# One ordered block for attention and experts, weight sums on VectorE, token copies on two engines

## The chip, the cores and the metric

The kernel runs on one core of a Trainium2 chip. A core has five engines with their own instruction lists: TensorE (PE, with its weight loads PEld), VectorE (DVE), ScalarE (ACT), GpSimd (POOL) and SyncE (SP, which here issues transfers). Each engine works through its list in order and waits on semaphores for the others.

The metric is the time of one execution on the device, in microseconds (us). Before the change it is 823.42 us, the median of three runs (822.31 to 827.64).

## The reference

An attention block feeds a mixture of experts, all in float32:

```python
# attention: 8 batches x 8 heads, 576 positions, head size 64, a sliding window of 128, a bias by distance
scores = q @ k.T / sqrt(64)
attn = softmax(where(0 <= rel < 128, scores - slope_h * rel, -1e9))
x = (attn @ v)              # laid out as 4608 tokens x 512
# experts: each token goes to the one expert with the largest logit
logits = x @ w_gate         # 512 x 8
expert = argmax(logits); gate = softmax(logits)[expert]
out[token] = gate * (relu(x[token] @ w1[expert]) @ w2[expert])   # w1: 512 x 1024, w2: 1024 x 512, per expert
```

## The kernel before

**Attention.** A loop over 32 steps (batch and pair of heads) computes scores on PE, exponentials on ACT, a product with a table of factors on DVE, sums of neighbouring blocks (`mg`) on POOL, and the values on PE. Tasks for the gate run beside it: they turn the logits, choose each token's expert (`pick`), give it a row number (`place`), and `scatter` writes the token's row to a list in memory by expert. The loop stands in a block of its own, `with tc.manual_schedule()`, inside which each engine's list follows the order of the program. What stands outside such a block, or in another one, may be ordered against it by the scheduler.

**Experts.** Each of the eight experts has a big group (512 tokens) and, between two experts, a small group (128 tokens) takes tokens that did not fit: big 0, small 0, big 1, small 1, up to big 7. A big group's two matrix products use Strassen's algorithm in the form with seven products and fifteen sums: `seven1` for w1 (two halves, seven products each), `seven2` for w2. It needs sums of the blocks of the weights (`w1_sums`, `w2_sums`: four instructions of 128 x 1024 each), of the tokens (`x_sums`) and of the hidden values (`left_sums` at the end of a half). Before the change the weight sums are on GpSimd:

```python
def left_sums(eng, s, a11, a12, a21, a22):
    eng.tensor_add(s[0], a21, a22)
    eng.tensor_sub(s[1], s[0], a11)
    eng.tensor_sub(s[2], a11, a21)
    eng.tensor_sub(s[3], a12, s[1])
# right_sums: the same with four subtractions
def w1_sums(g):
    ...
    left_sums(nc.gpsimd, ...)        # w2_sums: right_sums(nc.gpsimd, ...)

def seven(order, prod, post, banks):
    where = {1: 0, 2: 0, 6: 1, 5: 1, 3: 1, 7: 2, 4: 2}   # product -> PSUM bank a, b or c
    for n in order:
        prod(n, banks[where[n]], n in (1, 6, 7))         # PE, adds to what the bank holds
        post(n, *banks)                                  # DVE or ACT reads the bank

def post(n, ba, bb, bc):             # in seven1
    if n == 1:   nc.scalar.copy(p1[:], ba[:])
    elif n == 2: nc.scalar.activation(c11, ba[:], AF.Relu)
    elif n == 6: nc.vector.tensor_add(u2[:], bb[:], p1[:])
    elif n == 5: nc.vector.tensor_add(u4[:], bb[:], p1[:]); nc.vector.tensor_add(c22, bc[:], u4[:]); ...
    elif n == 3: nc.vector.tensor_add(c12, bb[:], p1[:]); ...
    elif n == 4: nc.vector.tensor_add(c21, bc[:], u2[:]); ...; left_sums(nc.vector, hs, c11, c21, c12, c22)
```

The gathered tokens (`xg`) are turned on PE, four transposes per tile of 128 tokens, into a PSUM tile `tp` that has two buffers, and copied to `xgT` by DVE:

```python
def tokens(g):                       # where each row of the group goes in the output: two small integer operations
    nc.vector.tensor_tensor(g["si"][:, :n], bits[:, :n, Dm], g["mask"][:, 0, :], op=ALU.bitwise_and)
    nc.vector.tensor_tensor(g["si"][:, :n], g["si"][:, :n], g["mask"][:, 1, :], op=ALU.bitwise_or)

def turn(g, tiles):
    for j in tiles:
        tp = pools["ps"].tile([P, DB, P], F32, name="tp")
        for db in range(DB):
            nc.tensor.transpose(tp[:, db, :], g["xg"][:, j, db * P : (db + 1) * P], ident[:])
        nc.vector.tensor_copy(g["xT"][:, :, j * P : (j + 1) * P], tp[:])
```

The loop over the groups (cut):

```python
def experts(first):
    ...
    g = groups[0]; gather(g); ...
    w1_sums(g)
    extras()                         # counts per expert, masks, lists of the small groups: 31 short DVE instructions
    get_w1(groups[1])
    for i, g in enumerate(groups):
        after = groups[i + 1 : i + 3] + [None, None]
        if after[0] is not None:
            gather(after[0]); after[0]["w2"] = load_w2(...)
        if g["n"] == NJ:             # a big group
            ...
            if i == 0:
                turn(g, [0, 1])
                # product 1 of both halves, product 2 of both halves
                turn(g, [2, 3]); x_sums(g)
                order = (6, 7, 5, 3, 4)
            w2_sums(g)
            for half in range(2):
                seven1(g, half, order, banks[half], us[half])
            if i == 0:
                check_range(first)
        else:
            layer1(g)                # a small group: plain products
        tokens(g)
        if after[1] is not None:
            get_w1(after[1])         # load the w1 of the group after the next
        if after[0] is not None:
            turn(after[0], range(after[0]["n"]))
            if after[0]["n"] == NJ:
                x_sums(after[0])
                w1_sums(after[0])    # on GpSimd, while a small group is worked on
        if g["n"] == NJ:
            seven2(g)
        else:
            layer2(g)

with moe_pools(), tc.manual_schedule():
    experts(True)
```

Of the kernel before, what the change touches and what calls it, by code (L numbers as in the profile page):

```python
# [8 lines left out]
F32 = mybir.dt.float32  # L9
# [12 lines left out]
def kernel(  # L22
# [310 lines left out]

# [7 lines left out]
    with tc.tile_pool(name="tab", bufs=1) as tab, \  # L346
# [230 lines left out]
                ts.append(lambda i=i: (send(tiles, i - 2), row(tiles, i)))  # L577
            return ts + [lambda: [send(tiles, i) for i in (len(tiles) - 2, len(tiles) - 1)]]

        with tc.manual_schedule():  # L580
            load(0)
            load(1)
            start_routing()
            tasks = []

            def do(n):
                for task in tasks[:n]:
                    task()
                del tasks[:n]

            for u in range(NU + 1):
                b, hp = divmod(u, HP)

                slow = u < 7
                if u < NU:
                    if hp == 1 and 1 < b + 1 < NB:
                        load(b + 1)
                    if 0 < u <= E:
                        clear_rows(u - 1)
                    if u == NU // 2:  # L600
                        expert_w[0] = load_w1(moe_w1[0]), load_w2(moe_w2[0])
                    scores(u)
                    factors(u, 0)
                do(0 if slow else 1)
                if u < NU:
                    factors(u, 1)
                    merge(u)
                if u > 0:
                    values(u - 1, 0)
                    values(u - 1, 1)  # L610
                    totals(u - 1)
                    if hp == 0:
                        tasks += tasks_of(b - 1)
                do(len(tasks) if u == NU else 0 if slow else 2 if len(tasks) < 14 else 3)

# [115 lines left out]
        return st  # L733

    def bank(i):
        return pools["ps"].tile([P, 2, TH], F32, name="abc"[i % 3])

    def left_sums(eng, s, a11, a12, a21, a22):
        eng.tensor_add(s[0], a21, a22)
        eng.tensor_sub(s[1], s[0], a11)  # L740
        eng.tensor_sub(s[2], a11, a21)
        eng.tensor_sub(s[3], a12, s[1])

    def right_sums(eng, t, b11, b12, b21, b22):
        eng.tensor_sub(t[0], b12, b11)  # L745
        eng.tensor_sub(t[1], b22, t[0])  # L746
        eng.tensor_sub(t[2], b22, b12)
        eng.tensor_sub(t[3], b21, t[1])

    def w1_sums(g):  # L750
        w1 = g["w1"]
        s = g["w1s"] = pools["s"].tile([P, 4, DH, F // 2], F32, name="w1s")
        f0, f1 = slice(0, F // 2), slice(F // 2, F)
        left_sums(
            nc.gpsimd, [s[:, i] for i in range(4)],
            w1[:, :DH, f0], w1[:, DH:, f0], w1[:, :DH, f1], w1[:, DH:, f1],
        )

    def w2_sums(g):
        w2 = g["w2"]  # L760
        t = g["w2s"] = pools["s"].tile([P, 4, FH, Dm // 2], F32, name="w2s")
        right_sums(
            nc.gpsimd, [t[:, i] for i in range(4)], w2[:, :FH, lo], w2[:, :FH, hi], w2[:, FH:, lo], w2[:, FH:, hi],
        )

    def seven(order, prod, post, banks):


        where = {1: 0, 2: 0, 6: 1, 5: 1, 3: 1, 7: 2, 4: 2}
        for n in order:  # L770
            prod(n, banks[where[n]], n in (1, 6, 7))
            post(n, *banks)

    def mms(out_of, lhs, rhs, nk, first):
        for i in range(2):
# [3 lines left out]
                    stop=(k == nk - 1), skip_group_check=True,  # L779
                )  # L780

    def seven1(g, half, order, banks, us):
        w1, s, xT, t, h, hs = g["w1"], g["w1s"], g["xT"], g["xTs"], g["h"], g["hs"]
        fs = [(2 * half + i) * P for i in range(2)]
        p1, u2, u4 = us
        r0, r1 = slice(2 * half, 2 * half + 2), slice(FH + 2 * half, FH + 2 * half + 2)
        c11, c12, c21, c22 = h[:, r0, lo], h[:, r0, hi], h[:, r1, lo], h[:, r1, hi]
        sides = {
            1: (lambda i, k: w1[:, k, fs[i] : fs[i] + P], lambda k: xT[:, k, lo]),
            2: (lambda i, k: w1[:, DH + k, fs[i] : fs[i] + P], lambda k: xT[:, DH + k, lo]),  # L790
            3: (lambda i, k: s[:, 3, k, fs[i] : fs[i] + P], lambda k: xT[:, DH + k, hi]),
            4: (lambda i, k: w1[:, DH + k, F // 2 + fs[i] : F // 2 + fs[i] + P], lambda k: t[:, 3, k, :]),
            5: (lambda i, k: s[:, 0, k, fs[i] : fs[i] + P], lambda k: t[:, 0, k, :]),
            6: (lambda i, k: s[:, 1, k, fs[i] : fs[i] + P], lambda k: t[:, 1, k, :]),
            7: (lambda i, k: s[:, 2, k, fs[i] : fs[i] + P], lambda k: t[:, 2, k, :]),
        }

        def prod(n, out_of, first):
            mms(out_of, *sides[n], DH, first)

        def post(n, ba, bb, bc):
            if n == 1:
                nc.scalar.copy(p1[:], ba[:])
            elif n == 2:
                nc.scalar.activation(c11, ba[:], AF.Relu)
            elif n == 6:
                nc.vector.tensor_add(u2[:], bb[:], p1[:])
            elif n == 5:
                nc.vector.tensor_add(u4[:], bb[:], p1[:])
                nc.vector.tensor_add(c22, bc[:], u4[:])  # L810
                nc.scalar.activation(c22, c22, AF.Relu)
            elif n == 3:
                nc.vector.tensor_add(c12, bb[:], p1[:])
                nc.scalar.activation(c12, c12, AF.Relu)
            elif n == 4:
                nc.vector.tensor_add(c21, bc[:], u2[:])
                nc.scalar.activation(c21, c21, AF.Relu)

                left_sums(nc.vector, [hs[:, i, r0, :] for i in range(4)], c11, c21, c12, c22)

        seven(order, prod, post, banks)

    def temps():
        return [pools["u"].tile([P, 2, TH], F32, name=n) for n in ("p1", "u2", "u4")]

    def seven2(g):
        w2, t, h, hs = g["w2"], g["w2s"], g["h"], g["hs"]
        p1, u2, u4 = temps()
        zo = g["zo"]
# [18 lines left out]

        def post(n, ba, bb, bc):
            if n == 1:  # L850
                nc.scalar.copy(p1[:], ba[:])
            elif n == 2:
                weigh(0, 0, ba)
            elif n == 6:
                nc.vector.tensor_add(u2[:], bb[:], p1[:])
            elif n == 5:
                nc.vector.tensor_add(u4[:], bb[:], p1[:])
                nc.vector.tensor_add(o[:, 1, 1], bc[:], u4[:])  # L858
                weigh(1, 1, o[:, 1, 1])
            elif n == 3:  # L860
                nc.vector.tensor_add(o[:, 0, 1], bb[:], p1[:])
                weigh(0, 1, o[:, 0, 1])
                send_out(g, 0, zo[:, 0, :])
                send_out(g, 1, zo[:, 1, :])
            elif n == 4:
                nc.vector.tensor_add(o[:, 1, 0], bc[:], u2[:])
                weigh(1, 0, o[:, 1, 0])
                send_out(g, 2, zo[:, 2, :])
                send_out(g, 3, zo[:, 3, :])

        seven((1, 6, 7, 5, 2, 3, 4), prod, post, [bank(i) for i in range(3)])

    def send_out(g, j, row):
        ins = nc.gpsimd.indirect_dma_start(  # L874
# [19 lines left out]
        nc.vector.tensor_tensor(g["si"][:, :n], bits[:, :n, Dm], g["mask"][:, 0, :], op=ALU.bitwise_and)  # L894
        nc.vector.tensor_tensor(g["si"][:, :n], g["si"][:, :n], g["mask"][:, 1, :], op=ALU.bitwise_or)  # L895

    def turn(g, tiles):
        if tiles[0] == 0:
            g["xT"] = pools["wk"].tile([P, DB, NJ * P], F32, name="xgT")
        for j in tiles:  # L900
            tp = pools["ps"].tile([P, DB, P], F32, name="tp")
            for db in range(DB):
                nc.tensor.transpose(tp[:, db, :], g["xg"][:, j, db * P : (db + 1) * P], ident[:])  # L903
            nc.vector.tensor_copy(g["xT"][:, :, j * P : (j + 1) * P], tp[:])  # L904

    def x_sums(g):
        xT = g["xT"]
        t = g["xTs"] = pools["wk"].tile([P, 4, DH, TH], F32, name="xTs")
        right_sums(
            nc.vector, [t[:, i] for i in range(4)], xT[:, :DH, lo], xT[:, :DH, hi], xT[:, DH:, lo], xT[:, DH:, hi],  # L910
        )

    def hidden(g):
        g["h"] = pools["wk"].tile([P, FB, NJ * P], F32, name="h_sb")
# [40 lines left out]
    def experts(first):  # L955
# [12 lines left out]
        else:  # L968
            get_w1(g)
            g["w2"] = load_w2(g["src"][1])  # L970
        w1_sums(g)
        extras()
        get_w1(groups[1])
        for i, g in enumerate(groups):
            after = groups[i + 1 : i + 3] + [None, None]
# [3 lines left out]
            if g["n"] == NJ:  # L979
# [2 lines left out]
                hidden(g)  # L982
                order = (1, 6, 7, 5, 2, 3, 4)
                if i == 0:
                    turn(g, [0, 1])
                    g["xTs"] = None
                    for half in range(2):
                        seven1(g, half, (1,), banks[half], us[half])
                    for half in range(2):
                        seven1(g, half, (2,), banks[half], us[half])  # L990
                    turn(g, [2, 3])
                    x_sums(g)
                    order = (6, 7, 5, 3, 4)
                w2_sums(g)
                for half in range(2):
                    seven1(g, half, order, banks[half], us[half])
                if i == 0:
                    check_range(first)
            else:
# [4 lines left out]
            if after[0] is not None:  # L1004
                turn(after[0], range(after[0]["n"]))
                if after[0]["n"] == NJ:
                    x_sums(after[0])
                    w1_sums(after[0])
            if g["n"] == NJ:
                g["zo"] = pools["wk"].tile([P, NJ, Dm], F32, name="zo")  # L1010
                seven2(g)
            else:
                layer2(g)

    with moe_pools(), tc.manual_schedule():
        experts(True)

    more = nc.values_load(n_more_i[0:1, 2:3], min_val=0, max_val=N * H + NX)
    with tc.If(more > 0):
# [52 lines left out]
```

## Time and profile before

| What | Before |
|---|---|
| time, median of 3 | 823.42 us |
| span of the profiled run | 821.3 us |
| PE busy | 723.7 us (88%) |
| DVE busy | 380.0 us (46%) |
| ACT busy | 207.6 us (25%) |
| POOL busy | 317.9 us (39%) |
| weight sums on POOL | 64 instructions of 128 x 1024, 2.35 to 2.37 us each |

A row of the profile names a line of the kernel, the engine, the operation, what it writes and reads, how often, and the mean duration; behind it stand the idle time of that engine just before and what ended it. The timeline gives one instruction, or a run of equal ones, per line, with its start and its length in us and the idle time before it in square brackets. "PEclk" is the share of TensorE's full clock that it was granted. Attention takes about the first 240 us, the experts the rest.

### The profile page before, as it was taken

The page shows a single profiled execution, that of the slowest core. Times are in us where ns is not written, and L with a number is a line of the kernel's source. Part 1 is how long each engine was busy: PE and PEld are TensorE (multiplying, and loading weights), DVE is VectorE, ACT ScalarE, POOL GpSimd, SP SyncE. Part 2 cuts the span into 40 slices and gives each one's busy share as a digit, 9 for nine tenths or more (in the row PEclk, how much of TensorE's full clock was granted, in tenths as well). Part 3 has the DMA queues.
Part 4 walks back from the last instruction along what each step waited for, and adds up shares of the span by engine and source line. Part 5 has one row for each costly group of instructions (what it writes and reads, how often), then busy time and mean ns, then how long its engine had stood idle before and what let it go on. Part 6 is the DMA issues. An engine that isn't in the chain of part 4 may idle for free.

```text
span 821.3 us, 11640 instructions
## 1 busy us (share of the span) xinstructions
PE 723.7 (88%) x4678; PEld 592.5 (72%) x4678; DVE 380.0 (46%) x655; ACT 207.6 (25%) x483; POOL 317.9 (39%) x250
## 2 busy tenths in 40 slices
PE   4998999998726888999899899989989989998992
PEld 3776777766525678688688678958868876885882
DVE  5467577776854423351542523245153333515330
ACT  4554455554301102121121121202102121210210
POOL 5445665666770005501640650352065055015401
PEclk9999899999957999999999999999999999999997
DMA  9995695531126024721832752272283247205001
GB/s 340 363 364 202 226 342 178 186 139 66 52 71 256 6 103 152 274 82 47 292 115 103 248 183 103 84 284 82 85 308 126 102 154 276 93 37 180 4 1 55
DMA packets 53615, 130.74 MB, mean 159 GB/s; under 512 B 3503, under 2 KB 3503, under 8 KB 53552
## 3 DMA queue, kind: packets, MB, share of 16 engines
q1 hardware_dynamic: 47024, 110.97, 38.9%
q0 software_dynamic: 6000, 18.92, 6.1%
q8 instruction: 39, 0.64, 0.3%
q14 instruction: 24, 0.20, 0.1%
q10 hardware_dynamic: 528, 0.02, 0.0%
HBM read 102.55 MB, written 28.12 MB: 159 GB/s over the span
## 4 chain that ended last, share of the span: by engine, by line
PE 54%; DVE 7%; issue 7%; POOL 2%; DMA 0%; POOLq 0%; DVEq 0%
PE b L777 18%; PE a L777 12%; PE c L777 12%; PE c L936 6%; PE a L923 2%; DVE si L895 2%; DVE si L894 2%; PE tp L903 2%; PE c L923 2%; PE b L923 2%; DVE xgT L904 1%; POOL out_dram L874 1%; POOL x_rows L173 0%; DMA x_rows<-xs,slots 0%; POOL w2s L745 0%
## 5 line engine op out<-in xcount | busy, mean ns | idle before, releaser
L874 POOL DMA_INDIRECT out_dram<-zo,si x32 | 31.5, 984 | 336.2 <-ACT zo L847 331.3
L442 POOL TENSOR_TENSOR mg<-probs 128x768 f32<-128x768 f32 x31 | 57.5, 1854 | 77.8 <-DVE probs L435 33.3
L423 ACT ACTIVATE e<-sp 128x512 f32<-128x512 f32 x128 | 66.4, 600 | 51.0 <-PE sp L416 46.5
L416 PE MATMUL sp<-q_sb,k_sb 64*128 64x256 f32 (+2 forms) x640 | 71.2, 367 | 6.3 <-DMA k_sb<-in_kT_dram 5.2
L416 PEld LDWEIGHTS sp<-q_sb,k_sb 64*128 64x128 f32 x640 | 62.4, 198 | 17.6 <-issue 5.4
L461 PE MATMUL m<-probs,v_sb 128*64 128x256 f32 (+3 forms) x768 | 64.9, 318 | 3.5 <-DVE probs L430 3.0
L430 DVE TENSOR_TENSOR probs<-e,fac 128x1024 f32<-128x1024 f32 x32 | 44.7, 1396 | 47.1 <-ACT e L423 31.7
L777 PE MATMUL a<-xgT,w 128*128 128x256 f32 x256 | 62.2, 389 | 3.3 <-DVE xgT L904 3.3
L461 PEld LDWEIGHTS m<-probs,v_sb 128*64 128x64 f32 x768 | 48.8, 139 | 20.6 <-DVE probs L430 3.4
L777 PE MATMUL b<-xTs,w1s 128*128 128x256 f32 x256 | 60.6, 380 | 3.0 <-DVE xTs L746 2.5
L903 PE MATMUL tp<-ident,xg 128*128 128x128 f32 x156 | 25.4, 307 | 40.1 <-DVE xgT L904 24.1
L777 PEld LDWEIGHTS a<-xgT,w 128*128 128x128 f32 x256 | 50.1, 196 | 13.9 <-DVE xgT L904 3.7
L777 PE MATMUL a<-w,h_sb 128*128 128x256 f32 x256 | 59.6, 387 | 0.0
L777 PE MATMUL b<-w2s,hs 128*128 128x256 f32 x256 | 57.9, 379 | 0.0
L936 PE MATMUL c<-w,h_sb 128*128 128x512 f32 x112 | 56.4, 662 | 0.0
L847 ACT ACTIVATE zo<-zo,xg 128x256 f32<-128x256 f32 x48 | 21.8, 500 | 136.5 <-DVE zo L858 89.4
L777 PEld LDWEIGHTS b<-xTs,w1s 128*128 128x128 f32 x256 | 48.5, 190 | 10.1 <-issue 2.7
L777 PEld LDWEIGHTS a<-w,h_sb 128*128 128x128 f32 x256 | 49.3, 195 | 6.8
L777 PEld LDWEIGHTS b<-w2s,hs 128*128 128x128 f32 x256 | 48.6, 190 | 6.6
L903 PEld LDWEIGHTS tp<-ident,xg 128*128 128x128 f32 x156 | 20.4, 158 | 43.7 <-DVE xgT L904 26.5
L173 POOL DMA_INDIRECT x_rows<-xs,slots x36 | 40.9, 1136 | 11.6 <-issue 5.4
L936 PEld LDWEIGHTS c<-w,h_sb 128*128 128x128 f32 x112 | 23.7, 217 | 27.9 <-issue 27.9
(191 smaller groups left out, 1259.2 us busy)
## 6 DMA issues: line engine op xcount, KB each, us to landing
w<-in_moe_w_dram SPq DMA_DIRECT2D x30, 2048.0 KB, 10.6
x_rows<-zero_row SPq DMA_DIRECT2D x8, 1028.0 KB, 14.4
xg<-x_rows SPq DMA_DIRECT2D x16, 514.0 KB, 6.3
v_sb<-in_v_dram SPq DMA_DIRECT2D x8, 1024.0 KB
q_sb<-in_qT_dram SPq DMA_DIRECT2D x7, 1152.0 KB
k_sb<-in_kT_dram SPq DMA_DIRECT2D x7, 1152.0 KB, 9.3
v_sb<-in_v_dram SPq DMA_DIRECT2D x8, 256.0 KB, 9.7
xg<-x_rows SPq DMA_DIRECT2D x7, 257.0 KB, 2.8
```

Source lines behind the costliest of these rows:

```text
L173: ins = nc.gpsimd.indirect_dma_start(out=x_d[:, :], out_offset=bass.IndirectOffsetOnAxis(ap=slots[:, t : t + 1], axis=0), in_=row, in_offs ...
L416: nc.tensor.matmul(sps[s][par][:, c : c + n], lhsT=k_sb[b][half, hp, k_lo[j] : k_lo[j] + P], rhs=q_sb[b][half, hp, q0 : q0 + n], start=Tru ...
L423: nc.scalar.activation(exps[u][s][:, par, :], sps[s][par][:], AF.Exp, scale=D ** -0.5)
L430: nc.vector.tensor_tensor(to.rearrange("p a (j c) -> p a j c", c=2 * P), e.rearrange("p a (j c) -> p a j c", c=2 * P), fac[:, heads, None, ...
L442: eng.tensor_add(mg[:, :, : 3 * P].rearrange("p a (t c) -> p a t c", c=P), two[:, :, :, 0, :], two[:, :, :, 1, :],)
L461: nc.tensor.matmul(xp[par * HALF : (par + 1) * HALF, lo - q0 : hi - q0], lhsT=v_sb[b][:, j, h * D : (h + 1) * D], rhs=probs[u][:, par, c + ...
L777: nc.tensor.matmul(out_of[:, i, :], lhsT=lhs(i, k), rhs=rhs(k), start=(first and i == 0 and k == 0), stop=(k == nk - 1), skip_group_check= ...
L847: nc.scalar.activation(o[:, th, dh, i, :], src[:, i, :], AF.Copy, scale=g["xg"][:, j, Dm + 1 :])
L874: ins = nc.gpsimd.indirect_dma_start(out=out[:, :], out_offset=bass.IndirectOffsetOnAxis(ap=g["si"][:, j : j + 1], axis=0), in_=row, in_of ...
L903: nc.tensor.transpose(tp[:, db, :], g["xg"][:, j, db * P : (db + 1) * P], ident[:])
L923: nc.tensor.matmul(hps[:, 0, :P], lhsT=g["w1"][:, db, fb * P : (fb + 1) * P], rhs=g["xT"][:, db, :P], start=(db == 0), stop=(db == DB - 1),)
L936: nc.tensor.matmul(zf, lhsT=g["h"][:, fb, :P], rhs=g["w2"][:, fb, :], start=(fb == 0), stop=(fb == FB - 1))
```

## The change

It has four parts. Attention and experts come into one ordered block, so that each engine's list follows the program from end to end. All weight sums go from GpSimd to VectorE, as lists of steps that are put between the readings of PSUM: w2's sums into the first half of `seven1`, after products 6, 7, 5 and 3, and w1's sums of the next big group into `seven2`, after products 5, 2, 3 and 4 (before, they ran while the small group was worked on). Turned tokens are copied by ScalarE for even tiles and by VectorE for odd ones. The third and fourth tile of a big group go through the PSUM buffers of the tags "a" and "b", not through `tp`. In the first big group the remaining tiles are turned between product 1 and product 2. The aim is that TensorE no longer waits for tokens between the groups.

```diff
+    order_all = ExitStack()
+    order_all.enter_context(tc.manual_schedule())
 ...
-        with tc.manual_schedule():
-            load(0)
+        load(0)                                  # (the whole loop of attention, one level out)
 ...
-    def left_sums(eng, s, a11, a12, a21, a22):
-        eng.tensor_add(s[0], a21, a22)
+    def left_sums(s, a11, a12, a21, a22):
+        v = nc.vector
+        return [
+            lambda: v.tensor_add(s[0], a21, a22), lambda: v.tensor_sub(s[1], s[0], a11),
+            lambda: v.tensor_sub(s[2], a11, a21), lambda: v.tensor_sub(s[3], a12, s[1]),
+        ]
 ...                                              # right_sums, w1_sums and w2_sums likewise
-    def seven(order, prod, post, banks):
+    def seven(order, prod, post, banks, more):
         for n in order:
             prod(n, banks[where[n]], n in (1, 6, 7))
             post(n, *banks)
+            run(more.get(n, ()))
 ...
-    def turn(g, tiles):
+    def turn(g, tiles, tags=("tp", "tp", "a", "b")):
 ...
-            tp = pools["ps"].tile([P, DB, P], F32, name="tp")
+            tp = pools["ps"].tile([P, DB, P], F32, name=tags[j])
 ...
-            nc.vector.tensor_copy(g["xT"][:, :, j * P : (j + 1) * P], tp[:])
+            copy = nc.scalar.copy if j % 2 == 0 else nc.vector.tensor_copy
+            copy(g["xT"][:, :, j * P : (j + 1) * P], tp[:])
 ...
-        w1_sums(g)
         extras()
+        run(w1_sums(g))
 ...
                 if i == 0:
                     turn(g, [0, 1])
                     for half in range(2):
-                        seven1(g, half, (1,), banks[half], us[half])
+                        seven1(g, half, (1,), banks[half], us[half], {})
+                    turn(g, [2, 3], ("tp",) * NJ)
+                    x_sums(g)
                     for half in range(2):
-                        seven1(g, half, (2,), banks[half], us[half])
-                    turn(g, [2, 3])
-                    x_sums(g)
+                        seven1(g, half, (2,), banks[half], us[half], {})
                     order = (6, 7, 5, 3, 4)
-                w2_sums(g)
-                for half in range(2):
-                    seven1(g, half, order, banks[half], us[half])
+                ws = w2_sums(g)
+                seven1(g, 0, order, banks[0], us[0], {6: ws[:1], 7: ws[1:2], 5: ws[2:3], 3: ws[3:]})
+                seven1(g, 1, order, banks[1], us[1], {})
 ...
                 if after[0]["n"] == NJ:
                     x_sums(after[0])
-                    w1_sums(after[0])
             if g["n"] == NJ:
-                seven2(g)
+                ws = w1_sums(after[1]) if after[1] is not None else []
+                seven2(g, {5: ws[:1], 2: ws[1:2], 3: ws[2:3], 4: ws[3:]})
 ...
-    with moe_pools(), tc.manual_schedule():
+    with moe_pools():
         experts(True)
+    order_all.close()
```

## The prediction

> **What bounds the kernel now.** I read the page's busy times first, then the groups with shapes kept apart, the waits, the timeline around one small group, and the timeline between attention and experts.
>
> ```profile
> PE 723.7 (88%) x4678; PEld 592.5 (72%) x4678; DVE 380.0 (46%) x655; ACT 207.6 (25%) x483; POOL 317.9 (39%) x250
> ```
>
> TensorE is busy for 88% of the span, and no product is added or removed. So the change can win only what PE waits, 821.3 - 723.7 = 97.6 us, and time in which PE runs at a lower clock. DVE has room: 46%. Which of PE's waits are touched? In the list of waits the largest of PE in the expert stage is this (us in total, times, longest):
>
> ```profile
> PE tp L903 <- DVE xgT L904: 24.1, 7, 3.6
> ```
>
> Seven times, once per small group, the third transpose of the next big group waits for DVE to copy a turned tile out of `tp`. Why is DVE late? The groups by shape, with mean ns after the comma:
>
> ```profile
> L740 POOL TENSOR_TENSOR w1s<-w1s,w 128x1024 f32<-128x1024 f32 x8 | 18.8, 2350 | 0.6
> L895 DVE TENSOR_TENSOR si<-si,xmasks 128x1 int32<-128x1 int32 x7 | 15.8, 2261 | 0.2
> L894 DVE TENSOR_TENSOR si<-xg,xmasks 128x1 int32<-128x1 int32 x7 | 15.0, 2147 | 0.0
> L894 DVE TENSOR_TENSOR si<-xg,masks 128x4 int32<-128x4 int32 x8 | 1.2, 156 | 0.2 <-issue 0.2
> ```
>
> The same small operation takes 156 ns in a big group and 2147 ns in a small one, with less data. A slow one lasts about as long as one weight sum on POOL. The timeline of the second small group (start, length) puts them side by side:
>
> ```profile
> 391.95 2.37 POOL L739 TENSOR_TENSOR w1s<-w 128x1024 f32<-128x1024 f32 x1
> ...
> 394.39 2.35 POOL L740 TENSOR_TENSOR w1s<-w1s,w 128x1024 f32<-128x1024 f32 x1
> ...
> 394.62 2.14 DVE L894 TENSOR_TENSOR si<-xg,xmasks 128x1 int32<-128x1 int32 x1
> ...
> 396.79 2.26 DVE L895 TENSOR_TENSOR si<-si,xmasks 128x1 int32<-128x1 int32 x1
> ...
> 398.98 1.28 DVE L904 COPY xgT<-tp 128x512 f32<-128x512 f32 x2
> ...
> 399.71 1.25 PE L903 MATMUL tp<-ident,xg 128*128 128x128 f32 x8 [3.57 <-DVE xgT L904]
> ```
>
> Each DVE operation ends when a POOL sum ends. The copies stand behind them, and PE stands 3.57 us.
>
> Between attention and experts it is the same at a larger scale:
>
> ```profile
> 224.18 2.06 DVE L142 TENSOR_TENSOR sel<-sc,mx 128x40 f32<-128x40 f32 x1
> 226.11 2.33 POOL L745 TENSOR_TENSOR w2s<-w 128x1024 f32<-128x1024 f32 x1
> 226.27 2.29 DVE L146 TENSOR_TENSOR_SCAN pre<-keep,sel 128x48 f32<-128x48 f32 x1
> ...
> 240.91 0.98 POOL L173 DMA_INDIRECT x_rows<-xs,slots  x1 [0.30 <-issue]
> 244.44 0.19 DVE L635 TENSOR_TENSOR has<-cnt,tail 128x32 f32<-128x32 f32 x1 [8.89 <-DMA x_rows<-xs,slots]
> ...
> 253.71 9.31 PE L777 MATMUL a<-xgT,w 128*128 128x256 f32 x32 [3.33 <-DVE xgT L904]
> ```
>
> The first expert's weight sums got ahead of attention's last five scatters on POOL, and slow the choice of experts on DVE too. The first expert product begins at 253.71.
>
> [...] the one `mg` sum on DVE (128x768) took 959. So I estimate 1.22 us for a weight sum on DVE, half of POOL's 2.35. [...] The window 470 to 472 us, just after one of the 3.57 us waits, shows a granted clock of 0.50; 402 to 404, after another, shows 1.00. So some of these waits cost a second time.
>
> **The change, part by part.**
>
> *Small groups.* From the first product of a small group to the first of the next big group PE takes 21.24, 19.71, 21.41, 20.99, 21.43, 20.98 and 21.41 us, 147.2 in all. What must be in it: eight blocks of `layer1` (387.96 to about 395.1), 7.1; sixteen transposes of 0.13 us, 2.1; `layer2`, 16 records at the full clock's 0.43 us, 6.9. That is 16.1. The rest is the wait of 3.5 and, in five or six of seven, a slow start of `layer2`. After the change no sum runs on POOL there, so L894 and L895 take 0.15 each, and transposes three and four have buffers of their own and wait for no copy. What comes next is the gather: a half lands 2.8 to 6.3 us after its issue, and it is issued 1.9 us into the small group. Half two may land at 8.2, where PE comes to it at 8.2. I allow 0.5 us. So 16.6 a group: 147.2 - 7 x 16.6 = **31.0 us saved**.
>
> *The sums on DVE.* Eight a big group of 1.22: 9.8 us, 78 us in all, on top of 380. In `seven1` a product takes 1.73 us. After product 6: `u2` 0.69, two sums 2.44, done in 3.3 with the semaphores, while products 7 and 5 take 3.46. `u4`, which product 3 waits for, so starts on time, and product 2 stands between. After 5: `u4`, `c22`, one sum, 2.8 against 3.46 for products 2 and 3. After 3: `c12` and a sum, 2.1 against 1.73: DVE falls 0.4 behind, and carries it through `left_sums` (2.7) to the next half's `u2`, which has 1.73 of slack less 0.9. So **0 us** on PE's path. In `seven2` a product takes 3.45, twice as long; w1 is loaded from its start, lands in 8.7 to 13.5 us, and the first sum comes at about 15. Also 0. The last expert adds nothing at the end: its w1 sums are gone long before.
>
> *Between attention and experts.* `lmin` is ready at 221.23 in both. From there to the first `xs` took until 228.74; in an earlier round without POOL's sums it took 1.57 us (202.82 to 204.39), so 222.8: 5.9 sooner. The second half loses one more blocked operation (L554, 1.72 against 0.14). Scatters start when the row numbers are there, about 224.3 in place of 235.64, and take the same 5.3 us to the last, 229.6 in place of 240.91: 11.3 sooner. `has`, which waits for the scatters, falls from 244.44 to 233.1. Then 31 instructions of `extras`, 8.0 us, to 241.2. Now the price: the four w1 sums stand behind them on DVE, 5.0 us, and the second tile's copy behind these, 0.7: product 1 starts at about 247.0, not 253.7. **6.7 saved** of 11.3.
>
> *First big group.* Tiles three and four are turned and summed while product 2 runs. From the first product to the first product 6 it took 12.7 us (253.71 to 266.38); now two times 4.65 for the products and 1.0 for the transposes, 10.4: 2.3 saved. Product 3 follows 5 at once in this group, so the sums make `u2` of half two some 0.5 late. **1.8 saved.**
>
> *Start.* In program order ACT makes the table of factors before its first exponentials, and the first `probs` comes perhaps 0.5 us later; the second one about as before. **0.3 lost.**
>
> Sum: 31.0 + 6.7 + 1.8 - 0.3 = 39.2. 823.4 - 39.2 = **784.2 us**.
>
> **Rivals.** (1) *DVE becomes the late engine*: 0.4 us behind in half one could grow if sums cost 1.4, as the 128x1024 products beside `mg` do (1396 ns). But these run beside POOL sums, which are gone in the expert stage. If PE waited 1 us in every `seven1`: 792. (2) *The gather takes the wait's place.* In the last small group the first transpose waited 0.72 for the gather already. If half two landed 2 us late in each: 16.6 becomes 18.2, and the time 795. Against it: the longest landing seen is 6.3. (3) *The clock does not recover*: idle may not be the only cause of 0.5. If 1 us a group stays: 791. (4) *Everything bites*: if PE has no wait in the small groups and the gather is free, 3.5 us more: 781; and if the weight sums found a gap before the scatters landed, 5 more.
>
> **Range and chances.** Rivals 1 to 3 pull up by 7 to 11 each, 4 down by 4 to 9; two together are possible, three hardly. 774 to 797. The 2% line lies at 807: past it lie only all three at once. Faster 0.95, same 0.04, slower 0.01.
>
> **What would show it.** Right: L900 and L901 on 128x1 near 0.16 us; no wait of `tp` or of banks a and b for `xgT`; the small groups at 16 to 17 us on PE with a clock of 1.00; weight sums on DVE at 1.22; the first expert product near 247; DVE about 408 busy (380 + 78 for the sums, less 29 of blocked L894 and L895, some 8 blocked before the experts, and 20 copies of 0.68 that go to ACT). Wrong: PE waits for `u4` or `u2` in `seven1`, or for `xg` in the small groups; a first product that is not earlier.

## The result and the profile after

The changed kernel takes 784.35 us (median of 4 runs, 783.84 to 785.33); the kernel before took 822.87 beside it. The ratio is 0.952, with a 95% interval from 0.948 to 0.956. The profiled run has a span of 782.3 us, against 821.3.

The page's busy times, as shown for the kernel before:

```profile
PE 711.7 (91%) x4678; PEld 587.7 (75%) x4678; DVE 405.3 (52%) x696; ACT 220.7 (28%) x506; POOL 175.8 (22%) x186
```

TensorE has the same 4678 products, 12 us shorter; VectorE has 25 us more work, GpSimd 142 less. PE's waits in the expert stage (us in total, times, longest):

```profile
PE tp L909 <- DMA xg<-x_rows: 10.7, 1, 10.7
...
PE a L783 <- DVE xgT L911: 7.5, 1, 7.5
...
PE a L909 <- DMA xg<-x_rows: 3.6, 6, 1.0
...
PE a L909 <- SPq L1027: 2.1, 1, 2.1
```

The first two rows are the waits ahead of the experts' first product: for the first gathered rows (15.2 us before), then for VectorE's copy of the second tile (3.3 before). The row of 24.1 us in seven waits for a copy is gone. In its place stand seven short waits ahead of the third tile: six for gathered rows, 3.6 in all, and one of 2.1 in the last small group that the profile puts down to SyncE's queue, which issues the gathers. The groups by shape:

```profile
L745 DVE TENSOR_TENSOR w1s<-w1s,w 128x1024 f32<-128x1024 f32 x8 | 9.8, 1225 | 0.3
...
L901 DVE TENSOR_TENSOR si<-si,xmasks 128x1 int32<-128x1 int32 x7 | 1.1, 159 | 0.2
...
L900 DVE TENSOR_TENSOR si<-xg,xmasks 128x1 int32<-128x1 int32 x7 | 1.0, 149 | 0.0
```

The two index operations of a small group fall from 2147 and 2261 ns to 149 and 159, and a weight sum takes 1225 ns on VectorE where it took 2350 on GpSimd. The timeline of the second small group:

```profile
380.28 0.15 DVE L900 TENSOR_TENSOR si<-xg,xmasks 128x1 int32<-128x1 int32 x1
...
380.76 1.04 PE L909 MATMUL tp<-ident,xg 128*128 128x128 f32 x8
...
382.78 0.63 PE L909 MATMUL a<-ident,xg 128*128 128x128 f32 x4 [0.98 <-DMA xg<-x_rows]
...
383.68 7.03 PE L941 MATMUL c<-w,h_sb 128*128 128x512 f32 x16
```

PE turns two tiles, waits 0.98 us for the second half of the gather, which had been issued at about 376.1 and landed after 6.7 us, turns the other two, and goes on at once. And between attention and experts:

```profile
229.63 0.97 POOL L173 DMA_INDIRECT x_rows<-xs,slots  x1 [0.30 <-issue]
...
233.16 0.19 DVE L638 TENSOR_TENSOR has<-cnt,tail 128x32 f32<-128x32 f32 x1 [5.82 <-DMA x_rows<-xs,slots]
...
241.15 1.22 DVE L745 TENSOR_TENSOR w1s<-w 128x1024 f32<-128x1024 f32 x1
...
245.82 0.68 DVE L911 COPY xgT<-tp 128x512 f32<-128x512 f32 x1
...
246.65 6.11 PE L783 MATMUL a<-xgT,w 128*128 128x256 f32 x16 [7.49 <-DVE xgT L911]
```

The last scatter leaves 11.3 us sooner than before (240.91), but the four weight sums now stand between the `extras` and the copy that the first product waits for; it starts 7.06 us sooner.

From the two timelines the 39.0 us of span come from three places. The seven small groups (first product of `layer1` to first product of the next big group) take 16.43, 16.93, 16.65, 16.52, 16.42, 16.36 and 18.01 us, 117.3 in all against 147.2: 29.9 saved. The start of the first small group moves from 317.93 to 308.40: 9.5 saved, 7.06 of it ahead of the first product and 2.5 inside the first big group. The end, behind the last product, gives 0.4 back. The big groups two to seven take 48.79 us each in both.

### The profile page after: what moved, and what is told of

The parts are those of the page before. It is cut to its first block, busy times and chain, and to the rows that moved or that the text cites. A ratio compares the mean times of both kernels' runs of the same rounds, so it can differ in the third digit from the quotient of the medians.

```text
span 782.3 us, 11598 instructions
## 1 busy us (share of the span) xinstructions
PE 711.7 (91%) x4678; PEld 587.7 (75%) x4678; DVE 405.3 (52%) x696; ACT 220.7 (28%) x506; POOL 175.8 (22%) x186
## 4 chain that ended last, share of the span: by engine, by line
PE 50%; issue 9%; DMA 5%; DVE 4%; POOL 1%; ACT 1%; SPq 0%; POOLq 0%; DVEq 0%
PE b L783 18%; PE a L783 13%; PE c L783 12%; PE c L941 5%; DMA xg<-x_rows 5%; ACT zo L853 1%; PE tp L909 1%; DVE zo L872 1%; POOL out_dram L880 1%; PE a L909 0%; DMA x_rows<-xs,slots 0%; PE b L909 0%; DVE hs L745 0%; DVE w1s L745 0%; DVE w1s L746 0%
## 5 line engine op out<-in xcount | busy, mean ns | idle before, releaser
L880 POOL DMA_INDIRECT out_dram<-zo,si x32 | 33.8, 1055 | 403.2 <-ACT zo L853 398.3
L420 PE MATMUL sp<-q_sb,k_sb 64*128 64x256 f32 (+2 forms) x640 | 73.0, 373 | 8.9 <-DMA k_sb<-in_kT_dram 5.0
L420 PEld LDWEIGHTS sp<-q_sb,k_sb 64*128 64x128 f32 x640 | 64.0, 202 | 20.5 <-issue 5.6
L434 DVE TENSOR_TENSOR probs<-e,fac 128x1024 f32<-128x1024 f32 x32 | 47.0, 1468 | 44.1 <-ACT e L427 29.3
L783 PEld LDWEIGHTS a<-xgT,w 128*128 128x128 f32 x256 | 50.2, 197 | 18.1 <-issue 11.2
L465 PE MATMUL m<-probs,v_sb 128*64 128x256 f32 (+3 forms) x768 | 63.2, 313 | 0.3 <-DVE xs L566 0.2
L941 PE MATMUL c<-w,h_sb 128*128 128x512 f32 x112 | 49.2, 592 | 0.0
L173 POOL DMA_INDIRECT x_rows<-xs,slots x36 | 43.4, 1205 | 19.6 <-DVE cnt L170 8.2
L439 DVE TENSOR_TENSOR probs<-e,fac 128x1024 f32<-128x1024 f32 x32 | 42.3, 1321 | 0.4 <-ACT e L427 0.4
L813 DVE TENSOR_TENSOR u<-b,p 128x512 f32<-128x512 f32 x16 | 11.1, 691 | 52.7 <-PE b L783 52.7
L941 PEld LDWEIGHTS c<-w,h_sb 128*128 128x128 f32 x112 | 20.7, 190 | 23.4 <-issue 23.4
```

The source lines that it names most:

```text
L173: ins = nc.gpsimd.indirect_dma_start(out=x_d[:, :], out_offset=bass.IndirectOffsetOnAxis(ap=slots[:, t : t + 1], axis=0), in_=row, in_offs ...
L420: nc.tensor.matmul(sps[s][par][:, c : c + n], lhsT=k_sb[b][half, hp, k_lo[j] : k_lo[j] + P], rhs=q_sb[b][half, hp, q0 : q0 + n], start=Tru ...
L434: nc.vector.tensor_tensor(to.rearrange("p a (j c) -> p a j c", c=2 * P), e.rearrange("p a (j c) -> p a j c", c=2 * P), fac[:, heads, None, ...
L439: nc.vector.tensor_tensor(to, e[:], fac2[:, heads, :], op=ALU.mult)
L465: nc.tensor.matmul(xp[par * HALF : (par + 1) * HALF, lo - q0 : hi - q0], lhsT=v_sb[b][:, j, h * D : (h + 1) * D], rhs=probs[u][:, par, c + ...
L783: nc.tensor.matmul(out_of[:, i, :], lhsT=lhs(i, k), rhs=rhs(k), start=(first and i == 0 and k == 0), stop=(k == nk - 1), skip_group_check= ...
```

## The experiments

**Theory.** Two things in series made the wait of a small group: index operations on VectorE that were blocked while GpSimd took weight sums (2147 and 2261 ns in before, each ending within 0.02 us of the end of a sum, against 149 and 159 in after), and only two `tp` buffers, so that PE's third transpose had to wait for the copies queued behind the blocked operations (24.1 us in seven). The order and the interleaving matter for what they put ahead of what PE waits for. **Rival:** the gain is that of the faster engine, VectorE, for the sums. Even where its code is unchanged, attention ends up to 3.6 us apart in the profiled runs (with the attention of after, the last scatter starts between 226.81 and 230.44), so the readings below are of stages wherever that is possible, not of absolute times.

**1. Before, with the copies alone changed.**

```diff
+    def turn(g, tiles, tags=("tp", "tp", "a", "b")):      # banks a and b for tiles 3 and 4
-            nc.vector.tensor_copy(...)
+            copy = nc.scalar.copy if j % 2 == 0 else nc.vector.tensor_copy
```

> The kernel before, with only the turned tokens changed: copies by ScalarE and VectorE in turn, tiles three and four through the buffers a and b. Weight sums stay on GpSimd, two ordered blocks. Theory (a wait with two causes in series, late VectorE and only two buffers of tp; to take away either one is enough): the two small integer operations still take 2.1 us each, but TensorE no longer waits for a copy; small groups 16.5 to 17.5 us in place of 21.0, the first product as late as before (253 to 254), time about 793 (790 to 798). Rival (a blocked VectorE holds up TensorE whatever the buffers): the wait moves to the next products, small groups stay at 20 or more, time 815 or more.

794.74 us, ratio 0.965 (0.962 to 0.968). The groups by shape of this run, and its wait:

```profile
L895 DVE TENSOR_TENSOR si<-si,xmasks 128x1 int32<-128x1 int32 x7 | 15.9, 2275 | 0.2
...
L894 DVE TENSOR_TENSOR si<-xg,xmasks 128x1 int32<-128x1 int32 x7 | 15.1, 2160 | 0.0
```

```profile
PE a L906 <- DMA xg<-x_rows: 5.2, 5, 1.5
...
PE a L906 <- ACT xgT L908: 0.3, 1, 0.3
```

The index operations are as slow as before, and the small groups take 117.2 us all the same. VectorE's own copies, of tiles two and four, still stand behind the blocked operations: in the second small group they start at 391.75 and 392.35. But PE has turned all four tiles by then, is at work on `layer2` from 390.07, and reads the copies only at 396.94. A blocked operation costs nothing where PE does not need soon what stands behind it. Which of the two, ScalarE or the further buffers, is enough was not tried.

**2. Before, with the index operations of a small group moved ahead of `layer1`.** GpSimd's sums start later, so that none runs beside them; buffers and engines stay.

```diff
             else:
+                tokens(g)
                 layer1(g)
-            tokens(g)
+            if g["n"] == NJ:
+                tokens(g)
```

> The kernel before, with the two small integer operations of a small group put ahead of its first layer, where no weight sum runs. Nothing is removed, no engine changes. Theory (they stand 2.1 us each behind GpSimd's sums, and the copies behind them): they fall to about 0.16 us, the wait of tp for xgT falls from 3.5 to under 1 a group, small groups 16.5 to 17.5, time about 794 (791 to 799). Rival (the two buffers of tp are the wait): the wait stays near 3.5, time 815 or more.

795.2 us, ratio 0.965 (0.963 to 0.968). From this run's groups by shape and its waits:

```profile
L895 DVE TENSOR_TENSOR si<-si,xmasks 128x1 int32<-128x1 int32 x7 | 1.1, 159 | 0.2
...
L894 DVE TENSOR_TENSOR si<-xg,xmasks 128x1 int32<-128x1 int32 x7 | 1.0, 149 | 0.0
```

```profile
PE tp L903 <- DVE xgT L904: 0.7, 2, 0.3
```

The small groups take 117.6 us. One moved call gives three quarters of the whole change's gain: 29.0 us against the kernel before beside it, of 38.5. Either remedy alone takes away all but 0.3 (run 1) or 0.7 (here) of the 24.1 us of waiting for copies; so in the changed kernel the two do not add up, since both remove the same wait.

**3. After, with all copies on VectorE through `tp`.**

```diff
-    def turn(g, tiles, tags=("tp", "tp", "a", "b")):
+    def turn(g, tiles, tags=("tp",) * 4):
-            copy = nc.scalar.copy if j % 2 == 0 else nc.vector.tensor_copy
+            copy = nc.vector.tensor_copy
```

> The changed kernel, with all copies of turned tokens by VectorE and all tiles through tp again. Theory (without blocked operations two buffers are enough; the gather's second half is what TensorE waits for): small groups 16.4 to 17.2, time 784 to 787. Rival (engines and buffers of the copies earned the gain in the small groups): a wait of about 3 us a group is back, time about 805.

784.26 us, ratio 0.952 (0.950 to 0.954): the same as after. In the profiled run the last small group takes 19.72 us instead of 18.01, the other six together 99.5 instead of 99.3. The copies' part of the change is worth nothing that the times show once the sums are off GpSimd.

**4. Before, with the one ordered block alone.**

```diff
+    order_all.enter_context(tc.manual_schedule())      # around attention and experts
-        with tc.manual_schedule():                     # attention's own
-    with moe_pools(), tc.manual_schedule():
+    with moe_pools():
```

> The kernel before, with only the one ordered block; weight sums stay on GpSimd, in the order of the program. Theory: the scatters now come ahead of the first weight sums on GpSimd and start near 224 in place of 235.6; but the w1 sums then run beside the 31 instructions of extras [...], so the first product begins at 247 to 252, not at 242, and the small groups stay at 21.0; time about 817 (813 to 821). Rival (order alone is what the part between attention and experts gained, nothing is lost to blocked extras): first product at 242, time about 812.

827.46 us, ratio 1.004 (1.002 to 1.006): 0.4% slower. I had expected a time of 813 to 821 and the first product at 247 to 252, and missed both; it came at 256.37. The timeline of this run:

```profile
232.90 2.34 DVE L638 TENSOR_TENSOR has<-cnt,tail 128x32 f32<-128x32 f32 x1 [6.20 <-POOL w1s L742]
...
235.15 2.34 POOL L744 TENSOR_TENSOR w1s<-w 128x1024 f32<-128x1024 f32 x1
235.28 2.25 DVE L632 TENSOR_SCALAR masks<-has 128x32 int32<-128x32 f32 x1
...
256.37 1.22 PE L780 MATMUL a<-xgT,w 128*128 128x256 f32 x2 [17.46 <-DVE xgT L907]
```

The scatters do go out at 224.2 to 229.4, as in after. But then all eight sums, w1's and w2's, run on GpSimd beside the `extras`, which take 22 us (232.90 to 255.0) where they took 8.0. I had reckoned with w1's four only. The small groups take 148.2 us, as before. The order moves the blocking from the scatters to the `extras`; it needs the sums off GpSimd to be worth anything.

**5. After, with the sums back on GpSimd at their new places.**

```diff
-        v = nc.vector                    # left_sums and right_sums of the weights
+        v = nc.gpsimd
```

> The kernel after, with the weight sums back on GpSimd (at the new, interleaved places of the program; order and copies stay those of after). Theory [...]: in the small groups the copies of turned tokens no longer queue behind the blocked index sums alone and have other banks, so the small groups stay at 16.4 to 17.4 us; but the extras between attention and experts are blocked as in the run of the order alone, since GpSimd takes w1's and w2's sums right behind the scatters: first product of the experts at about 255 us, not 246.65. Time about 793 (789 to 798). Rival (it is the engine VectorE itself, with shorter sums, that earns the gain of the small groups): the small groups go back to 20 to 21 us and the time is 812 or more.

789.79 us, ratio 0.960 (0.958 to 0.962). From its waits and its groups by shape:

```profile
PE a L781 <- DVE xgT L909: 16.9, 1, 16.9
```

```profile
L898 DVE TENSOR_TENSOR si<-xg,xmasks 128x1 int32<-128x1 int32 x7 | 7.7, 1107 | 0.0
```

The theory holds and the rival falls: with the other parts in place the engine is worth 5.4 us, not 38. The first product comes at 255.17 as expected (8.5 later than in after), and 9.5 us are lost by the start of the first small group. The small groups are even shorter than I expected, 112.9 us in all, five of them 15.76, against after's 117.3; this gives 4.4 back. The first of their index operations is blocked again (1107 ns; the second takes 159), and PE has no wait at all in five of them. The gather is issued 1.86 us into a small group in both, but GpSimd, busy with sums, sends the big group's last two scatters 1.2 to 1.4 us later (they start 3.07 and 4.37 us into the second small group, not 1.71 and 3.18), and the gather's second half lands sooner (at most 5.7 us after its issue, since PE comes to it then and does not wait; 6.7 in after). That these scatters held up the gather is argued from the times, not shown. Run 1 fits: GpSimd has the sums there too, but these scatters start at 1.71 and 3.00, and five small groups wait 0.5 to 1.5 us for rows. The last small group does not fit: here it waits 2.05 us with the late scatters as well.

**6. Before, with the sums on VectorE at the old places, in one lump.**

```diff
-            nc.gpsimd, [s[:, i] for i in range(4)],
+            nc.vector, [s[:, i] for i in range(4)],      # and w2's likewise
```

> The kernel before, with the weight sums on VectorE instead of GpSimd, at their old places in the program (all eight of an expert in one lump ahead of the first layer's products; order of the blocks and copies stay those of before). Theory: the two index sums of a small group take 0.15 us instead of 2.2 and the small groups fall to about 17 us (some 28 us in all); but VectorE takes w2's four sums in a lump ahead of the first left-side additions of the second layer's products, and PE waits for these some 2 to 3 us in each of the eight big groups (about 20 us). Time about 805 (798 to 815). Rival (the interleaving of the sums between PSUM readings is only tidiness): no new wait of PE in the big groups and the time is 785 to 795.

798.49 us, ratio 0.971 (0.968 to 0.973), at the low end of what I expected. The timeline of its second big group:

```profile
332.98 1.22 DVE L748 TENSOR_TENSOR w2s<-w,w2s 128x1024 f32<-128x1024 f32 x1
...
334.12 0.68 DVE L807 TENSOR_TENSOR u<-b,p 128x512 f32<-128x512 f32 x1
...
334.85 2.00 PE L777 MATMUL b<-xTs,w1s 128*128 128x256 f32 x8 [1.32 <-DVE u L807]
```

The lump ends 1.3 us too late, and a big group takes 50.37 us where it took 48.79. Seven of these and 6.1 us more in the first big group, less a first product 2.75 sooner, are the 14.4 us of span to after. I had put the wait at 2 to 3 us; it is 1.3 to 1.5. The small groups are 117.3 as in after. So the interleaving is what makes the sums free on VectorE. Against the kernel before, the engine alone gains 24.5 us here, in small groups that runs 1 and 2 shorten without it.

**7. After, with the first expert's w1 sums behind the first copies.**

```diff
         extras()
-        run(w1_sums(g))
 ...
                     turn(g, [0, 1])
+                    run(w1_sums(g))
```

> The kernel after, with one move: the first expert's four w1 sums stand behind the first copies of turned tokens instead of ahead of them. Theory: the sums (4 times 1.22 us on VectorE, 241.15 to 245.9) lie on the path to the experts' first product, though the first products do not read them; the first product comes 4.7 us earlier, at 241.9 instead of 246.65, and product 6 likewise. Time 779.6 (778.5 to 781). Rival (the first products would be held back by the weights' sums anyway, since the sixth product needs them): first product earlier, but product 6 at 255 to 257 and the time within 1 us of 784.3.

779.12 us, ratio 0.946 (0.943 to 0.949). First product at 241.62, product 6 at 250.88 instead of 256.92. The sums did lie on the path, without need.

**8. That, with the `extras` and the first gathers and loads of a small group behind the first big group's first layer.**

```diff
-        extras(); get_w1(groups[1])              # ahead of the first group
 ...
+                    extras(); get_w1(groups[1]); gather(after[0])     # behind seven1 of the first group
+                    after[0]["w2"] = load_w2(after[0]["src"][1]); range_sum(first)
 ...
+                    turn(after[0], range(after[0]["n"]))              # behind seven2 of the first group
+                    check_range(first)
```

> The run before this one, and besides it the index work of the extra (small) groups, the first of their gathers and loads, and the check of the range all move from ahead of the first big group to behind its first layer's products (the check's PE part behind its second layer's). Theory: nothing of them is needed by the first big group, so the first product comes at about 239.9 us, product 6 at about 250, and the wait of 4.6 us that PE has for the range's sum in the first group goes. Time about 775 (771 to 778). Rival (they only move: VectorE is then late for the first group's second-layer additions): PE waits 3 us or more for VectorE inside the first big group and the time is no lower than 779.

785.35 us, ratio 0.954 (0.952 to 0.956): 6 us slower than the run before, a miss. First product (237.0) and product 6 (247.5) came early as expected (4.6 us before run 7's, of which 2.6 are an earlier end of attention), and the wait for the range's sum went. But:

```profile
299.92 1.23 DVE L750 TENSOR_TENSOR w1s<-w 128x1024 f32<-128x1024 f32 x1 [13.48 <-DMA w<-in_moe_w_dram]
...
305.59 0.56 ACT L916 COPY xgT<-tp 128x512 f32<-128x512 f32 x1
...
306.20 2.08 PE L933 MATMUL a<-xgT,w 128*128 128x128 f32 x8 [10.30 <-ACT xgT L916]
```

Three loads of 2 MB were issued together, at 280.40, 282.15 and 282.63, and the last to land was the next expert's w1. VectorE takes its list in order: it stood 13.48 us before that expert's first sum. The readings of `zo` stand behind the sum, ScalarE's `zo` behind them, and the copy for the small group, which this edit put behind `seven2`, behind that. PE waited 3.1 us for `u` as well, as the rival said, and 10.3 us for this chain, which neither my theory nor the rival had.

**9. Run 7, with the range's sum ahead of the `extras`.**

```diff
+        range_sum(first)                 # three operations on VectorE, taken out of check_range
         extras()
```

> The run with the first w1 sums behind the first copies, and the range's sum on VectorE (three operations, 1.2 us) moved from behind the first expert's first layer to ahead of the extras, where VectorE waits 5.8 us for the scatters to land. Theory: the sum fills idle time there and the 4.6 us that PE waited for it goes; nothing else moves (the deferral of the extras, which that failed run tried as well, was the harmful part: it put the first w1 load of the next expert and what waits for it too late). Time 774.4 (773.4 to 775.8). Rival (the first w1 sums of the next expert, or the first h_sb, would hold PE at the same place anyway): a new wait of 2 us or more at the same place and the time 777 or more.

772.6 us, ratio 0.938 (0.934 to 0.942), 0.8 under the range. The gain is 6.5 us, more than the wait of 4.6. In run 7 the two lines were

```profile
275.81 0.56 PE L703 MATMUL tp<-n_in,ones_sq 128*128 128x1 f32 x2 [4.60 <-DVE n_in L701]
...
277.11 6.04 PE L783 MATMUL a<-w,h_sb 128*128 128x256 f32 x16
```

and here the wait is gone and the same sixteen products take less:

```profile
272.33 3.62 PE L788 MATMUL a<-w,h_sb 128*128 128x256 f32 x16
```

From product 6 to the first small group it is 52.83 in run 7 and 44.96 here: 7.9 us, 4.6 of wait and some 3 of the slow clock behind it. The row of run 7 for the stretch from 277.1 to 279.1 has the granted clock in its third column from the end, behind each engine's busy time (PE's comes first, with its number of products):

```profile
277.10:279.10 2.00, 2.00 (x7) 1.64 (x6) 0.16 (x1) 0.59 (x1) 0.00 (x0) 0.50 0.64 262
```

The clock is 0.50, with seven products in 2 us; in run 9 the first 2 us of the same products (from 272.3) have 1.00 and twelve. One thing was not as I thought: the sum did not fill VectorE's idle time. It started behind the landing of the scatters too, at 230.79, and the `extras` came 1.3 us later for it. Why it waited for the landing was not tried.

**10. Run 9, with the sums of all experts but the first on GpSimd.**

```diff
+        v = nc.vector if g["e"] == 0 else nc.gpsimd        # weight sums
```

> The run with the early range sum, with the weight sums of the second and all later experts on GpSimd and only the first expert's on VectorE. Theory: with nothing that PE waits for behind the index sums, GpSimd's sums do no harm there, and the small groups fall to 15.8 us as in the run of after with GpSimd's sums (its last scatters of the big group leave later, and the gather's second half lands sooner), while the stage before the experts stays as it is: 4.7 us less than the run before, 769.7 (768 to 771.5). Rival (VectorE is the better engine throughout, the 15.8 was due to that run's late start): small groups 16.4 or more, time 774 or more.

768.63 us, ratio 0.931 (0.927 to 0.935). PE's one wait in its small groups is

```profile
PE a L914 <- DMA xg<-x_rows: 1.6, 1, 1.6
```

The intervals of this run and the run before touch, but the stage is plain: small groups 112.1 us, six of 15.76 and one of 17.56, against 116.8. The rival falls: VectorE is not the better engine here.

**11. Run 9, sums on VectorE, with three buffers for gathered rows.**

```diff
-        pools["x"] = st.enter_context(tc.tile_pool(name="moe_x", bufs=2))
+        pools["x"] = st.enter_context(tc.tile_pool(name="moe_x", bufs=3))
```

> The run with the early range sum, sums on VectorE, with three buffers for the gathered rows instead of two. Theory (the gather waits for the buffer that the big group before holds until its last output): the gather is issued many microseconds earlier, PE's waits for gathered rows in the small groups (0.4 to 2.1 us in each of seven) go, and the small groups come to 15.8 us: about 769.5 (768 to 772). Rival (the gather sits behind the w load in the queue of SyncE, which itself waits for a buffer): the waits stay and the time is within 1.5 us of the run before.

764.92 us, ratio 0.928 (0.924 to 0.931), 3 us under the range. The gather for the third expert's rows in run 9:

```profile
363.72 0.90 SPq L900 DMA_DIRECT2D xg<-x_rows  x2
```

and here:

```profile
339.72 0.96 SPq L900 DMA_DIRECT2D xg<-x_rows  x2
```

It is issued 24 us sooner (23.9 us before the second small group begins, where in run 9 it is 1.86 us into it), and every small group takes 15.76 us, 110.3 in all: with no wait left, this is what PE needs. The groups account for 6.5 us; the medians of runs 9 and 11 differ by 7.7. My range stood on an expected 774.4 for run 9, which itself came out 1.8 lower.

**12. Run 10, with both of the first copies on ScalarE.**

```diff
-                    turn(g, [0, 1])
+                    turn(g, [0, 1], act=True)
```

> The run with later sums on GpSimd, and both copies of the very first turned tokens on ScalarE instead of one on each engine. Theory: the first product waited 2.8 us for VectorE, which reaches its copy only behind the extras; ScalarE is idle there, so the first product comes at about 239.3 instead of 241.6, product 6 follows only as far as VectorE's sums allow (w1 sums end about 246, the sums of turned tokens follow at 249 or so): 0.5 to 2 us less than the run before. Rival (VectorE's work ahead of product 6 is the bound by then): first product earlier, time the same within 0.5 us.

762.75 us, ratio 0.925 (0.921 to 0.928), the lowest of all, 21.6 us under after. PE's wait for copies ahead of the first product falls from 4.1 to 0.7 us, and product 6 comes 12.7 us behind the first transposes instead of 16.5, so VectorE was not the next bound, as the rival had it; I set the gain too low. Of 5.9 us between the medians these stages explain 3.8; the small groups take 1.0 more (113.2, the last one 18.60). In the profiled runs attention also ended 2.5 us sooner here, which the edit does not touch; this part stays open. Run 12 with three gather buffers was not tried.

## Why the prediction was right, point by point

- **Small groups: 31.0 us predicted, 29.9 measured.** The mechanism was right, the two causes in series are shown by runs 1 and 2. Two terms of the 16.6 were mis-sized and nearly cancel. What PE must do is 15.76 us, not 16.1 (run 11); the gather's wait is 0.8 us a group, not 0.5, since its second half lands up to 7.8 us after its issue, where I took 6.3 as the longest. A wait also costs some 0.2 more than its own length, which no term held (16.93 in the second small group, with a wait of 0.98).
- **Clock in small groups.** `layer2` takes 7.03 us in all seven; before, it took 7.03 in one and 7.61 to 8.73 in the other six, 7.2 us more in all. In the first 2 us of these six the granted clock was 0.57 to 0.71, and in the one of 7.03, behind a wait of 3.57 us, 1.00 (the waits of the six were 2.63 to 3.59). The waits did cost a second time in six of seven, as the text has it: 7.2 of the 29.9 us.
- **Sums on VectorE: 0 us on PE's path, right.** 1215 to 1225 ns against the 1.22 that was estimated. The 959 ns for 128x768 would give 1.28 in proportion; nearer is a product of 128x1024 on VectorE in before (L435, at 212.59), with no GpSimd sum beside it, which took 1.22 us. VectorE was busy for 405 us against some 408; there was no wait of a big group for `u2` or `u4` other than those that were there before. Run 6 shows how thin the margin is.
- **Between attention and experts: 6.7 predicted, 7.06 measured.** Scatters at 224.39 to 229.63 (224.3 and 229.6), `has` at 233.16 (233.1), end of `extras` 241.2 (241.2), first product 246.65 (247.0). That the times agree to 0.4 us is in part luck: the last scatter, which sets them, starts anywhere from 238.59 to 242.57 in runs with the attention and order of before (before, 1 and 2) and from 226.81 to 230.44 with those of after. Run 4 shows what the text did not say: without the move of the sums the order alone gains nothing here.
- **First big group: 1.8 predicted, 2.5 measured.** To product 6 it takes 10.27 us (10.4). The half microsecond that I took off for a late `u2` of half two did not show: PE waited 0.47 there, and 0.46 before.
- **Start: 0.3 lost predicted, nothing lost.** The first `probs` came at 15.34 instead of 13.93 us, later than the 0.5 I gave it, but attention's last values stand at 213.71 against 213.63. `lmin` was then ready at 220.47, 0.8 sooner than before, which I did not foresee and have not explained.
- **End: not in the sum.** From the last scatter to the end 11.5 us against 11.2.
- **Rivals.** (1) did not occur; run 6 is what it looks like. Its 792 stands for 1 us in every big group; a big group has two `seven1`, so 1 us in each of these would be 800. (2) occurred with 0.8 us of wait a group where it had 2. (3) did not. (4): run 11 got its first half by other means, 7.0 us instead of 3.5, and run 7 its 5 us, by moving the sums.

That the sum of 39.2 comes so close to a measured 39.0 of span is thus luck, better than its terms: the small groups gave 1.1 less, the first big group and the way to it (with the start) 1.3 more, and the end 0.4 less.

## What to carry to other kernels

Ask of a slow instruction what stands behind it on its engine before asking how to make it fast: two blocked operations of 2.2 us in each of seven small groups cost some 29 us in all where PE waited for the copies queued behind them and nothing where it did not, and moving one call gained 29.0 us where moving 64 sums to a faster engine (1.22 us a sum against 2.35) gained 24.5. Put side work that can be split between the readings that TensorE waits for, not in a lump ahead of them, and keep work that the next product does not read behind its copies. When a deferral moves loads, follow the engine that takes its list in order: one operation that waits for a late load (13.48 us in run 8) holds everything behind it.

## What the runs showed of the hardware

- An operation with one input was blocked too. In run 4 a `TENSOR_SCALAR` with one input of 128x32 took 2.25 us beside a GpSimd sum, against 0.17 for the one right behind it. It ends at 237.53, the GpSimd sum at 237.49. A `TENSOR_REDUCE` of 128x256, at 240.13 beside another sum, took 0.42, the same as without one in after. What decides which operations are blocked was not shown.
- A TensorE wait of 4.6 us cost 7.9 us in run 7: for about 5 us behind it the granted clock was 0.50, and sixteen products took 6.04 us instead of 3.62. The same wait cost 6.5 us in after, where the granted clock was 0.59 and 0.56 in the two stretches of 2 us from 281.9 on and the products took 5.04 (from product 6 to the first small group 51.48 us, against 44.96 without the wait). The length of the slow stretch differs from run to run; what sets it was not shown.
- A weight sum took 2.35 us on GpSimd and 1.22 on VectorE, and yet the kernel with later sums on the slower engine was no slower (768.63 against 772.6).
